# Spatial weights loaded from POOL's own queue, cast and subtraction in one step, and stacks held back around the change from z2 to z1

## The chip, the cores and the metric

The kernel runs on 1 core of a Trainium2 chip. The metric is device time in microseconds of one execution: before the change 1884.51 us, the median of 3 runs (1882.85 to 1885.61). The profile is of one further execution.

## The reference

The block adds attention and a gated MLP, both on the same layer norm, to its input. All data is fp32; S = 2048, D = 512, 32 heads of 16, F = 1792, Fh = 896.

```python
def _A_ref(x, wqkv, wo):                      # H = 32, Dh = 16
    q, k, v = split_heads(x @ wqkv)
    p = _softmax(jnp.einsum("bhqd,bhkd->bhqk", q, k) * (Dh ** -0.5))
    return merge_heads(jnp.einsum("bhqk,bhkd->bhqd", p, v)) @ wo

def _B_ref(x, w_in, w_sp, b_sp, w_out):
    z = _gelu(jnp.einsum("bsd,df->bsf", x, w_in))
    z1 = z[..., :Fh]
    z2 = _layernorm(z[..., Fh:], axis=-1)
    g = jnp.einsum("ts,bsf->btf", w_sp, z2) + b_sp[None, :, None]
    return jnp.einsum("bsf,fd->bsd", z1 * g, w_out)

xn = _layernorm(x)
return x + _A_ref(xn, A_wqkv, A_wo) + _B_ref(xn, B_w_in, B_w_sp, B_b_sp, B_w_out)
```

(`split_heads` and `merge_heads` stand for its reshapes.)

## The kernel before

Every fp32 operand is kept as a rounded part and a rest (`[128, 2, 512]`, fp32r), and a product is three matmuls. A raw weight of 128x512 is loaded, POOL casts it into the first part (L282) and subtracts that from the raw one into the second (L284).

After a start of some 125 us PE's work is written in 128 **rounds** by a `while` loop at the end of the kernel. Each round has 8 score slots (S, L1095; ACT takes their exponential, L71), 7 or 9 slots of maxima for a later head pair (M, L1109; DVE reduces each, L811), up to 27 **dense** slots (D, L1154), and one block of 32 values matmuls (V, L1192). A slot is a pair of matmuls on two halves of the array. The dense slots come from a queue in this order: v, q and k of the remaining heads, z2 (16 tiles of the second half of the MLP), z1 (its first half, 14 pairs), spatial (4 groups of 512 rows, each with 7 units over 16 weights wsp), mlp_out (with the 7 weights wout), attn_out (8 blocks of 24 slots with the weights wo). Where the loop's planner thinks that no dense slot is ready it writes a **filler** (F, L1168, products with zeros), or nothing.

The planner has a clock for PE and one each for ACT, DVE and POOL (`T["P"]`, `"A"`, `"D"`, `"G"`). A task is a generator: `yield "G", 0.61` books 0.61 us of POOL, and the instructions behind it are written when the planner's clock gets there; `"T"` is a delay (a load is taken to last LOAD = 5.0), `"C"` waits for a condition. So these numbers set the order of the instructions on every engine; how long things take on the chip does not enter. On the chip each engine takes its own instructions in order.

Buffers: a ring `big` of 19, for which the planner keeps leases; 3 of `hilo`; two accumulators in `dps` for the dense products, which the drain of a unit (L901 for attn_out) must read before the next may begin. At most DEEP = 4 raw weights are on their way at once. All transfers go out from SP (`move`, L125) in one order, but for the stores of xscr (L155), hscr (L722) and oscr (L870), which go out from POOL. `z2scr` holds z2 in DRAM; `zs` are its pieces, loaded again by SP for the spatial products. z1 is drained by ACT or DVE into `z`, to which POOL and ACT apply the gelu (L581 to L591, the tanh at L71). The outputs of the four groups of heads are normalized by `norm_out`: sums `os` (L851), their reciprocals stored to rscr and read back over all partitions (`ob`), POOL's products (L854, L858), the split (L864, L866) and the store to oscr. The last two head pairs' path ends in L934 to L956. `load_stacks` loads q and k of the next head pair.

Weights of one kind are asked for by `prepare`, which spawns a `weight` task for each.

Of the kernel before, what the change touches and what calls it, by code (L numbers as in the profile page):

```python
# [16 lines left out]
P = 128  # L17
# [5 lines left out]
NT = S // P  # L23
# [30 lines left out]
def fused_block(ctx, tc, x, wqkv, wo, w_in, w_spT, b_sp, w_out, out):  # L54
# [185 lines left out]
    def begin(nm, src, n, blocks=1, early=None):  # L240


        rw = piece(nm + "r").bitcast(F32)[:, 0, :n]
        dst, hi = rw, early
        if blocks > 1:
            src = src.rearrange("(c p) f -> p c f", p=P)
            dst = dst.rearrange("p (c f) -> p c f", c=blocks)
            hi = early and early[:, 0, :n].rearrange("p (c f) -> p c f", c=blocks)
        elif early:
            hi = early[:, 0, :n]  # L250
        move(dst, src)
        if early:
            nc.gpsimd.dma_start(hi, src)
        return rw
# [10 lines left out]
    def prepare(out, loads, spare=(0,)):  # L265
        for k, *a in loads:
            owed[0] += 1
            spawn(weight(out, k, a, spare), 1)
# [4 lines left out]
    def weight(out, k, a, spare):  # L273
        yield "C", lambda: raws[0] < DEEP and room["big"] > 1 + spare[0]
        raws[0] += 1
        rw = begin(*a)
# [4 lines left out]
        yield "G", 0.61  # L281
        nc.gpsimd.tensor_copy(t[:, 0, :n], rw)  # L282
        yield "G", 0.0026 * n
# [256 lines left out]
    def z2_all():  # L540
        yield from need(lambda: len(w2) == 2 * ND)
        for t in range(NT):
# [4 lines left out]
            if t == NT - 3:  # L547
                prepare(w1, [(f, f"w1_{f}", w_in[:, f * P:(f + 1) * P], D, ND) for f in range(NF)], spare=late1)
# [50 lines left out]
    def z1_all():  # L599
        for g in range(NG):  # L600
# [55 lines left out]
    def spatial():  # L656
        for n, (g, (x, y)) in enumerate(units):
# [7 lines left out]
            if lone:  # L665
                if g + 1 < NG:
                    prepare(wsp, [((g + 1, s), *sp_weights(g + 1, s)) for s in range(NT)])
                else:
                    prepare(wout, [(f, f"wout{f}", w_out[f * P:(f + 1) * P, :], 512) for f in range(NF)], spare=(2,))
# [118 lines left out]
    stacks = [0]  # L788

# [45 lines left out]
    def norm_out(g4, c):  # L835
# [16 lines left out]
        after(0.3, move, rscr[g4][c][:nh].rearrange("h (b x) -> h b x", x=32), sums[rows, 1, :])  # L852
# [124 lines left out]
    with tc.manual_schedule(engines=engines):  # L977
# [104 lines left out]
        def scores():  # L1082
# [5 lines left out]
            if p + 1 < NP and stacks[0] <= p and i >= (3 if p else 20) and (not owed[0] or i >= LATE):  # L1088
# [214 lines left out]
```

## Time and profile before

| | before |
|---|---|
| median of 3 runs | 1884.51 us (1882.85 to 1885.61) |
| the profiled execution | 1888.93 us, its span 1887.1 (1.8 lie around it) |
| mean granted clock of PE | 0.989 |
| PE busy | 1825.1 us (97%) |
| DVE, ACT, POOL busy | 1444.7, 1225.3, 690.7 us |
| DMAs issued by SP's and POOL's queues, share of the 16 engines | 50.6% and 4.8% |

A line of a group reads: line, engine, operation, out<-in with shapes and count, then busy us and mean ns of one, then the engine's idle time before it with what ended it. A row of a timeline reads: start, busy us, engine, line, operation, and in brackets the idle time just before. A row of a table by stretch reads: the stretch, its length, then busy us (and instructions) of the engines, the clock, the DMA share and GB/s. DMA lines end with the median us from issue to landing where the queue shows it. Buffer numbers are left out of names, so `wsp` is any spatial weight and `z` any of the MLP's first products.

### The profile page before, as it was taken

Reading aid. Unit: us, or ns where it says so; the run is one execution under the profiler, and the core shown is the slowest. Engines: PE = TensorE matmul, PEld = TensorE weight load, DVE = VectorE, ACT = ScalarE, POOL = GpSimd, SP = SyncE. Lnnn points to the kernel's source line nnn. Section 1 sums busy time; section 2 is a strip of 40 time slices with the busy share of each in tenths; the row PEclk is TensorE's granted clock in tenths of the full one; section 3 lists DMA queues with packets and bytes.
Section 4 is the critical chain, followed back from the end, with each engine's and each line's share of the span. In section 5 each row is a group of like instructions: output and inputs, shape, how many; then the busy total and the mean of one; then the engine's idle time right before and its main releaser. Section 6 shows DMA issues by size and latency. Waiting matters only on the chain.

```text
span 1887.1 us, 38105 instructions
## 1 busy us (share of the span) xinstructions
PE 1825.1 (97%) x14812; PEld 1109.3 (59%) x14812; DVE 1444.7 (77%) x1677; ACT 1225.3 (65%) x1338; POOL 690.7 (37%) x797
## 2 busy tenths in 40 slices
PE   6899999999998999999999999999999999999998
PEld 5665656566554656566655656565656565556554
DVE  5577878888876878778777877787778777878873
ACT  4247777888775777666656666666666665656555
POOL 2202142687886878800171217000722140002110
PEclk9899999999998999999999999999999999999999
DMA  9505573444455353474677657463787576456342
GB/s 329 208 3 170 203 225 111 98 137 118 133 160 160 129 130 110 141 167 119 158 201 194 165 142 227 133 148 103 219 194 160 161 201 145 124 140 174 116 129 92
DMA packets 208109, 291.47 MB, mean 154 GB/s; under 512 B 36008, under 2 KB 107368, under 8 KB 205048
## 3 DMA queue, kind: packets, MB, share of 16 engines
q1 hardware_dynamic: 197944, 258.03, 50.6%
q0 software_dynamic: 9984, 31.01, 4.8%
q8 instruction: 116, 1.90, 0.4%
q14 instruction: 65, 0.53, 0.1%
HBM read 186.98 MB, written 101.98 MB: 153 GB/s over the span
## 4 chain that ended last, share of the span: by engine, by line
PE 84%; DMA 4%; DVE 4%; POOL 4%; issue 2%; ACT 2%; SPq 0%; DVEq 0%; POOLq 0%; ACTq 0%
PE dps L1154 33%; PE sl L1192 22%; PE sl L1095 13%; PE sl L1109 12%; DVE mm L811 3%; DMA mscr<-ms 1%; PE dps L1168 1%; POOL wsp L284 1%; ACT pf L71 1%; DMA wqk<-in_wqkv 1%; PE sl L236 0%; PE sl L237 0%; DMA qst<-mscr 0%; PE sl L238 0%; ACT x L327 0%
## 5 line engine op out<-in xcount | busy, mean ns | idle before, releaser
L811 DVE TENSOR_REDUCE mm<-sl 128x2 f32<-128x1024 f32 x1024 | 1226.2, 1223 | 184.0 <-PE sl L1109 178.3
L71 ACT ACTIVATE pf<-sl 128x1024 f32<-128x1024 f32 x1024 | 1042.9, 1027 | 356.6 <-PE sl L1095 315.4
L1192 PE MATMUL sl<-pf,vall 128*32 128x512 f32 x4096 | 467.3, 597 | 0.0
L1095 PE MATMUL sl<-qst,kst 50*128 50x512 f32 x2048 | 441.4, 421 | 13.0 <-DVE mm L811 2.9
L1154 PE MATMUL dps<-wsp,zs 64*128 64x512 f32 x2688 | 441.4, 393 | 3.1 <-DMA zs<-z2scr 3.1
L1109 PE MATMUL sl<-kst,qst 48*128 48x512 f32 x2048 | 428.1, 408 | 7.2 <-DVE mm L811 3.5
L1095 PEld LDWEIGHTS sl<-qst,kst 50*128 50x128 f32 x2048 | 197.6, 185 | 223.8 <-issue 85.7
L1154 PEld LDWEIGHTS dps<-wsp,zs 64*128 64x128 f32 x2688 | 266.8, 187 | 41.5 <-DMA zs<-z2scr 3.7
L1192 PEld LDWEIGHTS sl<-pf,vall 128*32 128x32 f32 x4096 | 120.3, 110 | 270.6 <-issue 241.1
L1109 PEld LDWEIGHTS sl<-kst,qst 48*128 48x128 f32 x2048 | 197.6, 186 | 113.5 <-ACT pf L71 54.6
L1212 DVE TENSOR_TENSOR e<-sl,e 128x512 f32<-128x512 f32 x64 | 44.3, 692 | 174.3 <-PE sl L1192 133.8
L720 POOL TENSOR_TENSOR hhl<-z1i,hhl 128x512 fp32r<-128x512 f32 x28 | 35.8, 1290 | 332.3 <-ACT hhl L71 332.3
L71 ACT ACTIVATE e<-sl 128x512 f32<-128x512 f32 x64 | 38.3, 599 | 176.5 <-PE sl L1192 159.9
L1154 PE MATMUL dps<-w,xt 64*128 64x448 f32 x768 | 110.9, 369 | 2.3 <-ACT z L71 0.4
L1154 PE MATMUL dps<-wout,hp 64*128 64x512 f32 x672 | 111.5, 393 | 0.0
L858 POOL TENSOR_TENSOR ob<-ob 128x512 f32<-128x512 f32 (+1 forms) x16 | 20.6, 1288 | 181.9 <-DMA ob<-rscr 181.9
L1154 PEld LDWEIGHTS dps<-w,xt 64*128 64x128 f32 x768 | 73.9, 186 | 17.1 <-issue 8.0
L420 POOL TENSOR_TENSOR qkhl<-qr,qkhl 128x512 fp32r<-128x512 f32 x24 | 30.4, 1285 | 115.2 <-ACT qkhl L71 93.7
L1154 PEld LDWEIGHTS dps<-wout,hp 64*128 64x128 f32 x672 | 65.5, 187 | 9.1
L854 POOL TENSOR_TENSOR ob<-ob 128x512 f32<-128x512 f32 (+1 forms) x16 | 21.0, 1312 | 96.8 <-DMA ob<-escr 96.8
L1154 PE MATMUL dps<-xnT,wqk 64*128 64x512 f32 x288 | 47.4, 396 | 1.1 <-ACT vall L71 0.4
L1154 PE MATMUL dps<-wo,op 64*128 64x512 f32 x288 | 47.5, 407 | 0.6
(279 smaller groups left out, 1629.0 us busy)
## 6 DMA issues: line engine op xcount, KB each, us to landing
zs<-z2scr SPq DMA_DIRECT2D x192, 256.0 KB
escr<-e SPq DMA_DIRECT2D x60, 256.0 KB
hscr<-hhl POOLq DMA_DIRECT2D x28, 512.0 KB, 5.6
qst<-qscr SPq DMA_DIRECT2D x30, 384.0 KB
kst<-kscr SPq DMA_DIRECT2D x30, 384.0 KB
qscr<-qkhl SPq DMA_DIRECT2D x16, 512.0 KB
xscr<-xnT POOLq DMA_DIRECT2D x16, 512.0 KB, 4.5
kscr<-qkhl SPq DMA_DIRECT2D x16, 512.0 KB
```

What stands on the lines that cost most here:

```text
L71: return nc.scalar.activation(out, in_, func, **kw)
L284: nc.gpsimd.tensor_sub(t[:, 1, :n], rw, t[:, 0, :n].bitcast(F32))
L420: nc.gpsimd.tensor_sub(hl[:, 1, :], raw_, hl[:, 0, :].bitcast(F32))
L720: nc.gpsimd.tensor_sub(hl[:, 1, :], z1, hl[:, 0, :].bitcast(F32))
L811: nc.vector.tensor_reduce(mmax[g][:, :, t, kc], sl[k], AX.X, ALU.max)
L854: nc.gpsimd.tensor_add(both_[rows, 0, :], both_[rows, 0, :], both_[rows, 1, :])
L858: nc.gpsimd.tensor_mul(both_[rows, 0, :], both_[rows, 0, :], both_[rows, 1, :])
L1095: nc.tensor.matmul(sl[k][:, j, :], kst[p % 2][rows, kt * P:(kt + 1) * P], qst[p % 2][rows, c * 512:(c + 1) * 512], start=True, stop=True)
L1109: nc.tensor.matmul(sl[k][:, j, :], qst[p % 2][rows, tt * P:(tt + 1) * P], kst[p % 2][rows, kc * 512:(kc + 1) * 512], start=True, stop=True)
L1154: nc.tensor.matmul(dps[:, bank, :w], lhs, rhs, start=go, stop=stop)
L1192: nc.tensor.matmul(sl[k][cols:cols + VW, 0, :], vpack(kt + r, 2 * p + j), pf[:, j * 512:(j + 1) * 512], start=n == n_pv, stop=n == n_pv + ...
L1212: nc.vector.tensor_add(e, sl[k][:, 0, :], e)
```

## The change

Four edits. `weight` books the cast and the subtraction as one POOL step, so nothing comes between them; this holds for all prepared weights, w_in's too. Spatial weights of groups 1 to 3 and wout (55 loads) are loaded by `nc.gpsimd.dma_start`, with 0.7 us of POOL's clock for each, in place of SP's `move`. `calm` is off from z2's tile 13 to the second pair of z1, in which time stacks are loaded only from score step LATE = 24 on. The store of rscr in `norm_out` is due 1.5 us after its reciprocal in place of 0.3. The lines behind the edits move down by 3 to 7 (L282 is L286 after, L1095 L1102, L1109 L1116, L1154 L1161, L1168 L1175, L1192 L1199, L901 L908).

```diff
-    def begin(nm, src, n, blocks=1, early=None):
+    def begin(nm, src, n, blocks=1, early=None, put=None):
...
-        move(dst, src)
+        (put or move)(dst, src)
...
-    def weight(out, k, a, spare):
+    def weight(out, k, a, spare, own=False):
         yield "C", lambda: raws[0] < DEEP and room["big"] > 1 + spare[0]
         raws[0] += 1
-        rw = begin(*a)
+        if own:
+            lease("big", -1)
+            yield "G", 0.7
+            lease("big", 1)
+        rw = begin(*a, put=nc.gpsimd.dma_start if own else None)
         n = rw.shape[1]
         yield "T", LOAD
         yield open_("big")
         t = piece(a[0])
-        yield "G", 0.61
+        yield "G", 0.61 + 0.0026 * n
         nc.gpsimd.tensor_copy(t[:, 0, :n], rw)
-        yield "G", 0.0026 * n
         nc.gpsimd.tensor_sub(t[:, 1, :n], rw, t[:, 0, :n].bitcast(F32))
...
             if t == NT - 3:
+                calm[0] = False
                 prepare(w1, ...)
...
+                if n == 1:
+                    calm[0] = True
...
-                    prepare(wsp, [((g + 1, s), *sp_weights(g + 1, s)) for s in range(NT)])
+                    prepare(wsp, [((g + 1, s), *sp_weights(g + 1, s)) for s in range(NT)], own=True)
                 else:
-                    prepare(wout, ..., spare=(2,))
+                    prepare(wout, ..., spare=(2,), own=True)
...
+    calm = [True]
...
-        after(0.3, move, rscr[g4][c]..., sums[rows, 1, :])
+        after(1.5, move, rscr[g4][c]..., sums[rows, 1, :])
...
-            if p + 1 < NP and stacks[0] <= p and i >= (3 if p else 20) and (not owed[0] or i >= LATE):
+            if p + 1 < NP and stacks[0] <= p and i >= (3 if p else 20) and (i >= LATE or calm[0] and not owed[0]):
```

How the order moves, at three places. POOL, in the preparation of group 1's spatial weights, before; `wsp_3r` is the raw weight, `ob` and `z1i` belong to the norm and to a spatial result:

```order
L282 CAST wsp_3_10240<-wsp_3r 128x512
L284 TENSOR_TENSOR wsp_3_10240<-wsp_3r,wsp_3_10240 128x512
L282 CAST wsp_4_10314<-wsp_4r 128x512
L284 TENSOR_TENSOR wsp_4_10314<-wsp_4r,wsp_4_10314 128x512
L282 CAST wsp_5_10327<-wsp_5r 128x512
L282 CAST wsp_6_10346<-wsp_6r 128x512
L284 TENSOR_TENSOR wsp_5_10327<-wsp_5r,wsp_5_10327 128x512
L284 TENSOR_TENSOR wsp_6_10346<-wsp_6r,wsp_6_10346 128x512
L282 CAST wsp_7_10378<-wsp_7r 128x512
L858 TENSOR_TENSOR ob_0_9942<-ob_0_9942 128x512
L710 TENSOR_TENSOR z1i_6_10091<-z1i_6_10091,z1b_10374 128x512
L284 TENSOR_TENSOR wsp_7_10378<-wsp_7r,wsp_7_10378 128x512
```

And now (`hhl` is the split of a spatial result, hscr its store):

```order
L287 TENSOR_TENSOR wsp_3_10358<-wsp_3r,wsp_3_10358 128x512
L251 DMA wsp_4r<-in_w_spT 128x512
L251 DMA wsp_5r<-in_w_spT 128x512
L251 DMA wsp_6r<-in_w_spT 128x512
L251 DMA wsp_7r<-in_w_spT 128x512
L873 TENSOR_TENSOR ohl_0_10316<-ob_0_9913,ohl_0_10316 128x512
L877 DMA oscr<-ohl_0_10316 256x1x512
L716 TENSOR_TENSOR z1i_6_10193<-z1i_6_10193,z1b_10478 128x512
L286 CAST wsp_4_10504<-wsp_4r 128x512
L287 TENSOR_TENSOR wsp_4_10504<-wsp_4r,wsp_4_10504 128x512
L726 TENSOR_TENSOR hhl_6_10506<-z1i_6_10193,hhl_6_10506 128x512
L286 CAST wsp_5_10511<-wsp_5r 128x512
```

POOL now issues the loads in fours, between the subtraction of the last of one four and the cast of the first of the next.

ACT, where z1 begins, before: `z_0_0<-dps` drains z1's first product, `z2hl_0` rounds a piece of z2 into a `hilo` buffer, `pf` are exponentials:

```order
L71 ACTIVATE z2u_5768<-z2u_5768 128x896
L71 ACTIVATE pf_6112<-sl_188 128x1024
L71 ACTIVATE pf_6119<-sl_186 128x1024
L71 ACTIVATE pf_6129<-sl_187 128x1024
L71 ACTIVATE pf_6142<-sl_188 128x1024
L71 ACTIVATE pf_6154<-sl_186 128x1024
L71 ACTIVATE z2hl_0_6106<-z_14_5347,zrs_5757 128x512
L71 ACTIVATE pf_6163<-sl_187 128x1024
L71 ACTIVATE z_0_0_6165<-dps 128x512
```

And now:

```order
L71 ACTIVATE z2u_5768<-z2u_5768 128x896
L71 ACTIVATE z_0_0_6102<-dps 128x512
L71 ACTIVATE pf_6110<-sl_187 128x1024
L71 ACTIVATE pf_6122<-sl_188 128x1024
L71 ACTIVATE pf_6132<-sl_186 128x1024
L71 ACTIVATE pf_6150<-sl_187 128x1024
L71 ACTIVATE pf_6165<-sl_188 128x1024
L71 ACTIVATE pf_6182<-sl_186 128x1024
L71 ACTIVATE pf_6197<-sl_187 128x1024
L71 ACTIVATE pf_6214<-sl_188 128x1024
L71 ACTIVATE z_0_0_6102<-z_0_0_6102 128x512
L71 ACTIVATE z2hl_0_6181<-z_14_5347,zrs_5757 128x512
```

The drain stands seven rows earlier, ahead of the z2 piece and of the exponentials.

PE, the beginning of round 63, in the change from group 0 to 1, before:

```order
L1095 MATMUL sl_188<-qst_91,kst_93 128x512 x2
L1109 MATMUL sl_187<-kst_92,qst_90 128x512 x2
L1154 MATMUL dps<-wsp_0_10219,zs_10676 128x512 x6
L1154 MATMUL dps<-wsp_1_10225,zs_10676 128x512 x2
L1095 MATMUL sl_186<-qst_91,kst_93 128x512 x2
```

And now, where wsp_8 of the same group is the first that this round uses:

```order
L1102 MATMUL sl_187<-qst_91,kst_93 128x512 x2
L1116 MATMUL sl_188<-kst_92,qst_90 128x512 x2
L1175 MATMUL dps<-brow,zeror 128x512 x2
L1102 MATMUL sl_186<-qst_91,kst_93 128x512 x2
L1175 MATMUL dps<-brow,zeror 128x512 x4
L1116 MATMUL sl_187<-kst_92,qst_90 128x512 x2
L1102 MATMUL sl_188<-qst_91,kst_93 128x512 x2
```

Fillers stand where dense slots stood. In all, dense slots and fillers by round (other rounds up to 102 have at most 3 slots of difference, the same work overall):

| rounds | before: D (F) | after: D (F) |
|---|---|---|
| 30–34 | 2, 22, 8, 16, 24 (14, 0, 0, 0, 0) | 6, 18, 13, 15, 20 (12, 0, 7, 0, 1) |
| 46–52 | 25, 9, 10, 27, 26, 25, 24 (1, 7, 7, 1, 0, 0, 1) | 25, 9, 3, 12, 24, 24, 25 (2, 5, 10, 6, 1, 0, 0) |
| 62–69 | 24, 24, 24, 25, 24, 24, 24, 25 (1, 0, 0, 0, 1, 0, 0, 0) | 25, 9, 11, 17, 27, 27, 27, 27 (2, 7, 6, 3, 0, 0, 0, 0) |
| 77–81 | 24, 24, 25, 24, 24 (0, 0, 0, 1, 0) | 22, 12, 12, 27, 24 (2, 6, 6, 0, 0) |
| 92–99 | 24, 25, 24, 24, 24, 25, 24, 24 (2 in all) | 25, 9, 12, 16, 27, 27, 27, 27 (3, 8, 5, 4, 0, 0, 0, 0) |
| 123–127 | 17, 27, 4, 19, 18 (4, 0, 8, 3, 0) | 24, 24, 24, 24, 24 (none) |
| behind the last V | 11 (7) | 72 (7) |

mlp_out (21 slots a round) begins in round 103 before and 107 after, attn_out in 119 and 123. SP's rows go from 914 to 859, POOL's from 794 to 849; the stores of rscr and the loads of the stacks stand among the other rows of SP around z2's end as before.

More of the change, by code (lines that the diff above doesn't have):

```diff
@@ L851, in norm_out @@
         nc.vector.reciprocal(sums[rows, 1, :], sums[rows, 0, :])
-        after(0.3, move, rscr[g4][c][:nh].rearrange("h (b x) -> h b x", x=32), sums[rows, 1, :])
+        after(1.5, move, rscr[g4][c][:nh].rearrange("h (b x) -> h b x", x=32), sums[rows, 1, :])
         yield "G", 1.3
```

6 lines of the change are left out of this document (3 added, 3 removed).

## The prediction

> **What bounds the kernel now.** First the page: engine shares, the chain that ended last, and the costliest groups.
>
> ```profile
> PE 1825.1 (97%) x14812; PEld 1109.3 (59%) x14812; DVE 1444.7 (77%) x1677; ACT 1225.3 (65%) x1338; POOL 690.7 (37%) x797
> PE 84%; DMA 4%; DVE 4%; POOL 4%; issue 2%; ACT 2%; SPq 0%; DVEq 0%; POOLq 0%; ACTq 0%
> L811 DVE TENSOR_REDUCE mm<-sl 128x2 f32<-128x1024 f32 x1024 | 1226.2, 1223 | 184.0 <-PE sl L1109 178.3
> L1154 PE MATMUL dps<-wsp,zs 64*128 64x512 f32 x2688 | 441.4, 393 | 3.1 <-DMA zs<-z2scr 3.1
> ```
>
> PE holds 84% of the chain, and POOL is busy 37% of the span. So the edits on POOL pay only where PE waits for POOL's product, or where they change PE's own order. They do change it: the planner of the kernel reckons its order from costs of POOL steps. I therefore cut the trace at the ends of the 128 rounds and compare stretches. First, what a round costs when its dense slots are few (view: busy time by stretch, PE alone):
>
> ```profile
> 776.49:789.15 12.66, 12.32 (x98) 1.00 0.30 96
> 789.15:803.01 13.86, 13.65 (x104) 1.00 0.49 144
> 803.01:817.51 14.50, 14.38 (x122) 1.00 1.01 176
> 817.51:831.40 13.89, 13.89 (x122) 1.00 0.58 155
> 998.40:1011.38 12.98, 12.98 (x110) 1.00 0.34 93
> 1011.38:1025.04 13.66, 13.66 (x120) 1.00 1.02 210
> ```
>
> The first round has 7 maxima, 9 dense slots and 7 fillers, the second 9, 10 and 7; the third 7 maxima, 27 slots and a filler, the fourth 9 and 26. The last two are full rounds of 24 slots with 7 and 9 maxima. A round with 9 slots is only 0.3 us shorter than one with 24: the eight maxima on DVE (1223 ns each by L811's row) set a floor. **Dense slots that the planner leaves out of a round are thus not saved, they are postponed.** Prices from here: 12.7 to 13.0 (7 maxima) and 13.7 to 13.9 (9) for up to 25 slots; 13.6 and 14.1, my choice beside the 14.50 and 13.89 above, for 27.
>
> **Where PE now waits.** The worst stretch, rounds 30 to 34, and the change from spatial group 0 to 1, rounds 62 to 69 (columns: length, then busy us of PE, PEld, DVE, ACT, POOL, clock, DMA share):
>
> ```profile
> 533.76:613.09 79.33, 70.92 (x499) 36.17 (x496) 56.24 (x68) 49.98 (x57) 61.93 (x82) 0.89 0.54 152
> 762.07:858.50 96.43, 95.63 (x781) 55.91 (x778) 74.11 (x83) 61.36 (x65) 37.48 (x40) 1.00 0.56 142
> 978.89:1091.85 112.96, 109.56 (x908) 67.02 (x905) 85.52 (x98) 70.10 (x72) 29.62 (x30) 0.98 0.66 175
> 1186.31:1252.91 66.60, 66.46 (x563) 41.00 (x563) 50.55 (x53) 43.82 (x45) 4.19 (x4) 1.00 0.58 138
> 1387.99:1495.67 107.68, 107.41 (x904) 65.79 (x904) 85.53 (x98) 70.22 (x72) 24.01 (x23) 1.00 0.70 174
> 1806.42:1874.66 68.24, 64.27 (x534) 35.42 (x527) 29.87 (x36) 40.64 (x43) 6.24 (x6) 0.97 0.31 98
> 1874.66:1887.10 12.44, 7.46 (x72) 4.22 (x68) 7.77 (x8) 0.00 (x0) 0.00 (x0) 0.97 0.45 169
> ```
>
> What stands behind the first (timelines of SP, POOL, ACT, PE):
>
> ```profile
> 522.68 0.51 SPq L125 DMA_DIRECT2D w_0r<-in_w_in  x1
> 532.05 0.32 SPq L125 DMA_DIRECT2D rscr<-os  x1
> 532.47 1.06 SPq L125 DMA_DIRECT2D w_1r<-in_w_in  x1
> 568.62 0.68 POOL L870 DMA_DIRECT2D oscr<-ohl  x1
> 574.93 0.60 ACT L71 ACTIVATE z<-dps 128x512 f32<-128x512 f32 x1 [5.21 <-issue]
> 575.58 1.65 PE L1154 MATMUL dps<-xnT__5663,w 64*128 64x512 f32 x6 [4.44 <-ACT z L71]
> ```
>
> SP stands still between w_0r and w_1r, behind the rscr store; the weights reach POOL late, POOL's oscr store goes out at 568.62, and z_0_0 on ACT, whose buffer that store must free, starts at 574.93. PE waits 4.44 us. At 984 it is the z2 pieces and SP's queue:
>
> ```profile
> 986.76 0.50 PE L1154 MATMUL dps<-wsp,zs 64*128 64x512 f32 x1 [2.66 <-DMA zs<-z2scr]
> 988.07 1.49 PE L1154 MATMUL dps<-wsp,zs 64*128 64x512 f32 x6
> SPq L125 <- POOL wsp L284: 17.2, 7, 3.8
> ```
>
> The last row is SP's waits from 940 to 1000: in seven of them, 17.2 us, a raw load waited for a buffer that POOL's subtraction frees, and the zs loads queued behind it. This is what the loads on POOL's queue take away.
>
> **The change part by part, in time.** All differences are against the profiled execution (1888.93 us, 4.4 over the median of 1884.51); I carry the difference over to the median.
>
> *Rounds 30 to 34.* SP's order there is the same in both, rscr between w_0r and w_1r included, so that 9.4 us gap (522.68 to 532.05) stays, and with it the late POOL; the store moved by 1.2 us on the planner's clock changes nothing here. What goes is z_0_0's wait: ACT now has it seven rows earlier, on a buffer that is free; the z2 piece behind it takes the wait over, and late next are the exponentials behind that piece. By shape the five rounds now cost 13.9+12.9+13.9+12.7+13.7 = 67.1. Of the PE idle time in round 32 (6.57 us, 22.52 less the 15.95 in the row below) I leave half, 3.3: 70.4, that is **−8.9** (bounds −12.2 with no wait left, 0 if all stays).
>
> ```profile
> 560.68:583.20 22.52, 15.95 (x86) 0.70 0.90 224
> 565.12 0.66 PE L1095 MATMUL sl<-qst,kst 50*128 50x512 f32 x2 [0.48 <-DVE mm L811]
> 566.25 0.80 PE L1095 MATMUL sl<-qst,kst 50*128 50x512 f32 x2
> ```
>
> A part of that stretch is a slow clock, 0.70. The Trainium skill ("TensorE: Matmul & The Clock Gate", section "Why this matters for your kernels") says that TensorE drops to half rate after idle gaps of about 3 us, and advises to keep gaps shorter; by this the clock comes back with the gap of 4.44 us removed. The rows say something else: pairs take 0.66 and 0.80 us at 565 and 566, before that gap, and at 988 three slots take 1.49 after a gap of only 2.66. If the slowness stays, 30% of 15.95, 4.8 us, must be taken off the gain, which lies within the bound of 0 above: 1889.8 in place of 1885.
>
> *Rounds 46 to 52* lose 24 slots to later (D 9, 3, 12 in rounds 47 to 49): 14.4+12.7+13.9+12.8+13.7+13.0+13.9 = 94.4 for 96.43, **−2.0**. *Rounds 62 to 69* (25, 9, 11, 17, then four of 27): 13.9+12.7+13.9+12.9+14.1+13.6+14.1+13.6 = 108.8 for 112.96, **−4.2**: the wait at 984 goes, PE does fillers instead. *Rounds 77 to 81*: 66.7 for 66.60, **+0.1**. *Rounds 92 to 99*: as 62 to 69 but 14.1 for the first, 109.0 for 107.68, **+1.3**; nothing was waiting there. *Rounds 103 to 122*: the wout rounds stand four later, **−0.9** from the shorter attn_out rounds that leave.
>
> *The end.* Rounds 123 to 127 have 24 slots each and no late ob any more: 13.3+13.4+3×12.6 = 64.5 for 68.24, **−3.7**. But behind the last values block stand 72 dense slots, not 11:
>
> ```profile
> 1798.51 4.26 DMA ob<-rscr
> 1855.61 0.70 PE dps L1154 x6
> 1874.73 1.14 PE sl L949 x8
> 1879.44 1.23 DVE fin L901
> ```
>
> Three slots take 0.70, so 61 more take 14.2. The two accumulators of dps are read by L901 (1.23 us) between the blocks of 24, and there is nothing left to hide that: L949 (1.14) covers the first change, the second costs some 2 with its latencies. **+16.2**, bounds +14.2 and +19.
>
> *POOL's steps and loads.* Prices:
>
> ```profile
> 947.38 0.61 POOL L282 CAST wsp<-wsp_0r 128x512 fp32r<-128x512 f32 x1 [4.94 <-DMA wsp_0r<-in_w_spT]
> 948.08 1.29 POOL L284 TENSOR_TENSOR wsp<-wsp_0r,wsp 128x512 fp32r<-128x512 f32 x1
> 942.42 0.37 SPq L125 DMA_DIRECT2D wsp_0r<-in_w_spT  x1
> L722 POOL DMA_DIRECT2D hscr<-hhl x28 | 24.5, 890 | 0.7 <-POOL hhl L720 0.6
> hscr<-hhl POOLq DMA_DIRECT2D x28, 512.0 KB, 5.6
> oscr<-ohl POOLq DMA_DIRECT2D x12, 512.0 KB, 4.4
> wqk<-in_wqkv POOLq DMA_DIRECT2D x2, 256.0 KB, 9.9
> ```
>
> Cast and subtraction back to back take 2.0 us (947.38 to the end of the second at 949.37). 55 issues at 0.89 add some 49 us to POOL's 690.7, in idle time. But POOL works in order: four loads, four pairs, four loads. No load of the next four can go out until the pairs are done, and hhl's subtraction, the hscr store and ob stand behind a pair that waits for its load; spatial results wait for a hilo buffer there. One batch takes one issue, one landing and four pairs: 0.89+5.6+8.0 = 14.5 us with hscr's landing. The planner allots 0.7+5.0+4×1.94 = 13.5, so POOL falls 1 us behind its order in each batch, 4 us in a group of four batches. A landing like oscr's 4.4 or SP's own (942.42 to 947.38, 5.0) costs 0 to 1.6; one like wqk's 9.9, the only row with loads of this size on this queue, but from the kernel's start, would cost over 20 us a group. I take hscr's, the nearest in load, and a quarter of its 4 us, since fillers stand ahead of most batches' first use: **+3** in three groups; wout, two batches behind a long spatial unit, at 0.
>
> The Trainium skill ("DMA: Bandwidth & Descriptors", section "Latency and other measured facts") gives a first byte after some 1 us on GpSimd's software path against 0.6 on SP's; its section "Issuing engines are not separate DMA queues" says that all share the same 16 engines, so that another issuer saves only issue time. Added to SP's 5.0 that estimate is a landing of 5.4, and the term falls to about +2, 1884. The medians 4.4 and 5.6 lie on both sides of it.
>
> *Calm* moves no row: the stacks stand at the same place in SP's order, 0.
>
> Sum: −8.9−2.0−4.2+0.1+1.3−0.9−3.7+16.2+3 = +0.9, so 1889.8 for the profiled run and **1885** for the median. Put shortly: PE's order has 168 filler slots for 120, and 48 of them (11.2 us at 0.233) cost about what the waits that go were worth.
>
> **Rivals.** (1) *Faster.* The z_0_0 wait goes whole (−3.3) and weights are never late (−3): **1879**. For it speaks that the wait has one cause and that ACT's order removes it; against it the SP gap that stays. (2) *Slower: POOL's own loads are late.* With a DMA share of 0.66 to 0.70 in the changes of group, landings of 6.5 us give 1.9 a batch, 7.6 a group; half reaches PE, 11.4 for 3: **1893**. It decides from a landing of about 6 us on. For it speaks the wqk row, against it the two stores' medians. (3) *The stall of rounds 30 to 34 stays*, because POOL is as late as before and the next ACT row blocks as long: the −8.9 falls away, **1894**. (4) *The change doesn't do what it says*: SP's zs loads are late for other reasons, and PE waits at the same places as well as filling: the −4.2 and half of the −2.0 fall away, **1890**.
>
> **Chances.** Within 0.2% (3.8 us, about what a measurement of this kernel can tell from no change) is the forecast's own case, 1881 to 1888: 0.37. Rival 1: 0.28, all of it faster. Rival 2: 0.20, rival 3: 0.09, rival 4: 0.06, all slower: 0.35. The range takes rival 1 with the bound of no wait at all, 1876, and rivals 2 and 3 with the tail's upper bound, 1896.
>
> **What would show it.** Right: no gap above 3.3 us before L1154's successor (L1161) around 575; fillers (L1175) in rounds 63 to 65 and no wait for zs; last values block about 15 us earlier against the end than now, 28 to 29 us before it rather than 12.4; POOL's load issues of 0.7 to 0.9 us and landings near 5.6. Wrong: PE waits for wsp with POOL's cast as releaser above 1 us a group (rival 2), z_0_0's wait merely renamed (rival 3), or short rounds that really are shorter than 12.7, since then the postponed slots cost less than I charge.

## The result, and the profile after

| | before | after |
|---|---|---|
| median | 1885.06 us (1882.85 to 1887.52, 4 runs) | 1905.73 us (1903.06 to 1907.86, 4 runs) |
| ratio to before | | 1.0103 [1.0091, 1.0116] |
| profiled execution, its span | 1888.93, 1887.1 us | 1907.86, 1906.1 us |

The changed kernel is slower by 1.03%, about 20 us, where the prediction said no change (1885) with a range up to 1896. From the page of after, the engines, the chain, and two groups (the spatial products and the fillers):

```profile
PE 1843.6 (97%) x14908; PEld 1109.5 (58%) x14908; DVE 1440.9 (76%) x1677; ACT 1221.5 (64%) x1338; POOL 721.9 (38%) x852
PE 84%; DMA 5%; DVE 4%; POOL 2%; issue 2%; ACT 2%; SPq 0%; DVEq 0%; POOLq 0%; ACTq 0%
...
L1161 PE MATMUL dps<-wsp,zs 64*128 64x512 f32 x2688 | 437.4, 394 | 5.2 <-POOL wsp L286 3.9
...
L1175 PE MATMUL dps<-brow,zeror 64*128 64x512 f32 x336 | 62.4, 398 | 1.3 <-ACT z L71 0.7
```

The shares say almost nothing: PE is still 84% of the chain, POOL still under 40% busy. Two details speak. The spatial products, which before waited 3.1 us for z2's pieces, now wait for POOL's cast (`wsp L286`). And 336 filler matmuls, 168 slots, are in PE's order, as the forecast counted; the dense slots that they displaced were not saved but postponed.

Cut at the ends of the rounds, as in the prediction (before its numbers stand there; lengths in us, all from the profiled executions):

| rounds | before | after | difference | forecast |
|---|---|---|---|---|
| 30–34 | 79.33 | 78.72 | −0.6 | −8.9 |
| 46–52 | 96.42 | 93.73 | −2.7 | −2.0 |
| 62–69 | 112.96 | 119.34 | +6.4 | −4.2, and a share of +3 |
| 92–99 | 107.68 | 113.22 | +5.5 | +1.3, and a share of +3 |
| 103–122 | 269.88 | 269.66 | −0.2 | −0.9 |
| 123–127 | 68.24 | 66.68 | −1.6 | −3.7 |
| behind round 127 | 12.44 | 29.40 | +17.0 | +16.2 |

The rows by stretch of after: rounds 30 to 34, 62 to 69, and what lies behind round 127 (columns as before: length, PE, PEld, DVE, ACT, POOL, clock, DMA share):

```profile
531.29:610.00 78.71, 71.92 (x510) 37.04 (x506) 56.04 (x68) 48.87 (x55) 63.87 (x85) 0.93 0.55 151
972.96:1092.30 119.34, 113.18 (x893) 65.25 (x890) 83.74 (x96) 68.54 (x71) 49.94 (x55) 0.97 0.66 177
...
1876.70:1906.10 29.40, 22.98 (x194) 15.37 (x190) 10.14 (x10) 0.00 (x0) 0.00 (x0) 0.97 0.36 121
```

**Rounds 30 to 34.** ACT, then PE, in after:

```profile
577.14 0.81 ACT L71 ACTIVATE z2hl<-z,zrs 128x512 fp32r<-128x512 f32 x1 [3.81 <-DMA oscr<-ohl]
...
578.38 0.57 ACT L71 ACTIVATE e<-sl 128x512 f32<-128x512 f32 x1
```

```profile
575.56 0.63 PE L1161 MATMUL dps<-xnT__5665,w 64*128 64x512 f32 x4
579.00 0.50 PE L1102 MATMUL sl<-qst,kst 50*128 50x512 f32 x2 [2.81 <-ACT e L71]
```

z_0_0 no longer waits. The row behind it, `z2hl`, waits for the same oscr store (3.81 us), the exponential `e` stands behind it on ACT, and PE waits for that. The wait was renamed and moved one round on. How far one profiled execution can be trusted here: the kernel before and the two kernels with memsets below have the same order of instructions on every engine up to the end of round 34, and the five rounds took 79.33, 78.44 and 80.68 us.

**Round 63.** POOL in after, at the change from group 0 to 1:

```profile
958.47 1.27 POOL L865 TENSOR_TENSOR ob<-ob 128x512 f32<-128x512 f32 x1 [5.82 <-DMA ob<-rscr]
...
983.32 1.28 POOL L287 TENSOR_TENSOR wsp<-wsp_7r,wsp 128x512 fp32r<-128x512 f32 x1
984.55 0.58 POOL L251 DMA_DIRECT2D wsp_8r<-in_w_spT  x1
...
995.20 1.26 POOL L861 TENSOR_TENSOR ob<-ob 128x512 f32<-128x512 f32 x1 [8.46 <-DMA ob<-escr]
996.41 0.61 POOL L286 CAST wsp<-wsp_8r 128x512 fp32r<-128x512 f32 x1
...
1019.60 1.28 POOL L287 TENSOR_TENSOR wsp<-wsp_15r,wsp 128x512 fp32r<-128x512 f32 x1
```

and PE:

```profile
997.07 2.15 PE L1161 MATMUL dps<-wsp,zs 64*128 64x512 f32 x6 [3.91 <-POOL wsp L286]
```

In fours, as the order showed: wsp_8 is asked for at 984.55, when before POOL was about to finish the last one:

```profile
986.67 1.27 POOL L284 TENSOR_TENSOR wsp<-wsp_15r,wsp 128x512 fp32r<-128x512 f32 x1
```

In after, wsp_15 is done at 1020.88 (1019.60 and 1.28), 33 us later than the 987.94 of before. Between load and cast of wsp_8 stands an `ob` product, which holds POOL for 8.46 us until its read has landed; the weight lies ready behind it and PE stands. The first four of the group stood behind such a row too (958.47, 5.82 us). POOL is not busy in these two waits, it is held by its order.

**The end.** PE behind the last values block, in after:

```profile
1888.08 2.34 PE L1161 MATMUL dps<-wo,op 64*128 64x512 f32 x18
1890.26 0.85 PE L1161 MATMUL dps<-wo,ohl 64*128 64x512 f32 x6
1892.43 2.35 PE L1161 MATMUL dps<-wo,op 64*128 64x512 f32 x18 [1.33 <-DVE fin L908]
```

72 dense slots stand here instead of 11. Nine slots take 2.34, 0.26 each, so 61 more take 15.9, and the change of accumulator costs 1.33 at L908: 17.2 for a measured 17.0.

### The profile page after: what moved, and what is told of

Its sections match the earlier page's. It is cut to its first block, busy times and chain, and to the rows that moved or that the text cites. A ratio compares the mean times of both kernels' runs of the same rounds, so it can differ in the third digit from the quotient of the medians.

```text
span 1906.1 us, 38247 instructions
## 1 busy us (share of the span) xinstructions
PE 1843.6 (97%) x14908; PEld 1109.5 (58%) x14908; DVE 1440.9 (76%) x1677; ACT 1221.5 (64%) x1338; POOL 721.9 (38%) x852
## 4 chain that ended last, share of the span: by engine, by line
PE 84%; DMA 5%; DVE 4%; POOL 2%; issue 2%; ACT 2%; SPq 0%; DVEq 0%; POOLq 0%; ACTq 0%
PE dps L1161 34%; PE sl L1199 22%; PE sl L1102 13%; PE sl L1116 12%; DVE mm L818 3%; DMA zs<-z2scr 1%; PE dps L1175 1%; DMA kst<-in_wqkv 1%; DMA ob<-escr 1%; DMA oscr<-ohl 1%; DMA qst<-qscr 1%; ACT pf L71 1%; ACT x L330 0%; DMA rscr<-os 0%; POOL w L287 0%
## 5 line engine op out<-in xcount | busy, mean ns | idle before, releaser
L1199 PE MATMUL sl<-pf,vall 128*32 128x512 f32 x4096 | 467.7, 597 | 0.1
L1102 PE MATMUL sl<-qst,kst 50*128 50x512 f32 x2048 | 440.9, 423 | 13.1 <-DVE mm L818 3.6
L1161 PE MATMUL dps<-wsp,zs 64*128 64x512 f32 x2688 | 437.4, 394 | 5.2 <-POOL wsp L286 3.9
L1116 PE MATMUL sl<-kst,qst 48*128 48x512 f32 x2048 | 426.3, 409 | 7.9 <-ACT pf L71 3.7
L1102 PEld LDWEIGHTS sl<-qst,kst 50*128 50x128 f32 x2048 | 195.6, 184 | 229.3 <-issue 87.5
L1161 PEld LDWEIGHTS dps<-wsp,zs 64*128 64x128 f32 x2688 | 261.4, 187 | 48.9 <-POOL wsp L286 4.3
L1199 PEld LDWEIGHTS sl<-pf,vall 128*32 128x32 f32 x4096 | 120.4, 110 | 271.6 <-issue 243.8
L1116 PEld LDWEIGHTS sl<-kst,qst 48*128 48x128 f32 x2048 | 196.0, 185 | 117.4 <-ACT pf L71 63.5
L1161 PE MATMUL dps<-w,xt 64*128 64x448 f32 x768 | 110.7, 369 | 2.3 <-ACT z L71 0.4
L1161 PE MATMUL dps<-wout,hp 64*128 64x512 f32 x672 | 111.4, 392 | 0.0
L1161 PEld LDWEIGHTS dps<-w,xt 64*128 64x128 f32 x768 | 73.5, 186 | 17.5 <-issue 8.0
L1161 PEld LDWEIGHTS dps<-wout,hp 64*128 64x128 f32 x672 | 65.5, 187 | 8.9
L1175 PE MATMUL dps<-brow,zeror 64*128 64x512 f32 x336 | 62.4, 398 | 1.3 <-ACT z L71 0.7
L1161 PE MATMUL dps<-xnT,wqk 64*128 64x512 f32 x288 | 47.3, 396 | 1.1 <-ACT vall L71 0.4
```

The source lines that it names most:

```text
L1102: nc.tensor.matmul(sl[k][:, j, :], kst[p % 2][rows, kt * P:(kt + 1) * P], qst[p % 2][rows, c * 512:(c + 1) * 512], start=True, stop=True)
L1116: nc.tensor.matmul(sl[k][:, j, :], qst[p % 2][rows, tt * P:(tt + 1) * P], kst[p % 2][rows, kc * 512:(kc + 1) * 512], start=True, stop=True)
L1161: nc.tensor.matmul(dps[:, bank, :w], lhs, rhs, start=go, stop=stop)
L1175: nc.tensor.matmul(dps[:, bank, :], zeror[r:r + 64], brow[r:r + 64], start=not begun, stop=not begun)
L1199: nc.tensor.matmul(sl[k][cols:cols + VW, 0, :], vpack(kt + r, 2 * p + j), pf[:, j * 512:(j + 1) * 512], start=n == n_pv, stop=n == n_pv + ...
```

## The experiments

POOL is the engine that the theories differ on. One says that in the changes of group POOL's time sets when PE gets its weights, so that each load issued on POOL costs PE time; the others put the loss on late landings, on the order in which POOL is written, or on the stall of rounds 30 to 34. Below, "merge" is the cast and the subtraction booked as one step, and a "late slot" is a dense slot behind the last values block. All ratios are to the kernel before on the same chip, whose medians were 1885.2 to 1886.3 us.

### Without the loads on POOL's queue

```diff
-    prepare(wsp, [...], own=True)
+    prepare(wsp, [...])
-    prepare(wout, [...], spare=(2,), own=True)
+    prepare(wout, [...], spare=(2,))
```

> All of the change but the loads on POOL's own queue: SP issues every raw load again. PE's order has 134 filler slots (120 before, 168 with the whole change) and no dense slot behind the last values block (11, 72). Theory 1, the time goes into postponed dense slots, since the booked POOL step in front of each load lets the loads go out only in fours behind the casts: the tail's 17 us and the waits of rounds 63, 67 and 97 go, 1877 to 1886. Theory 2, it goes into the single step of cast and subtraction, which holds up the rest of POOL's queue: still above 1895.

1885.6 us, 0.9996 [0.9983, 1.0009]. As the first theory had it. Merge, calm and the later rscr together make no difference that can be measured; the 20 us belong to the loads on POOL and the step booked for them. The end is short again: there are 134 fillers, and no late slot; behind round 127 lie 12.88 us. Rounds 62 to 69 take 110.03 us (119.34 with the loads) and rounds 92 to 99 106.50 (113.22). But the stall of round 32 is in round 33 here too, so it does not come from the loads:

```profile
575.70:598.34 22.64, 17.89 (x97) 9.23 (x94) 9.50 (x11) 12.09 (x15) 15.09 (x22) 0.70 0.57 154
```

The merge itself gives and takes: rounds 62 to 74 are 3.0 us shorter than before, 75 to 102 are 7.6 longer, since SP's loads now wait for whole pairs on POOL (10.6 us for `wsp L287` from 1340 to 1391) and zs behind them.

### Loads on POOL, with no booked step ahead of them

```diff
-        if own:
-            lease("big", -1)
-            yield "G", 0.7
-            lease("big", 1)
```

> The whole change, but a load on POOL's queue is written at once when the planner asks for it, without the booked step of 0.7 and without waiting for POOL's clock. POOL's order then has a load behind each pair of cast and subtraction, not four behind four; PE's order is that of the kernel without own loads (134 fillers, none of the dense slots in the tail). Theory 1 (order): 1873 to 1884, since SP's waits for POOL at the change of groups go as well. Theory 2 (landings on POOL's own queue are late, 6 us and more): PE waits for wsp at each change of groups, 1890 to 1900.

1910.66 us, 1.0133 [1.0118, 1.0148]. The planner no longer knows of POOL's issue time, there are no fours, 134 fillers and no late slots, and it is worse than the change and above both expectations. The loss now lies in the waits of the three changes of group (rounds 62 to 74, 75 to 88, 89 to 102):

```profile
974.42:1164.24 189.82, 180.47 (x1479) 110.23 (x1475) 139.22 (x159) 112.63 (x117) 64.24 (x71) 0.97 0.70 176
1164.24:1362.82 198.58, 192.05 (x1589) 117.08 (x1585) 147.73 (x162) 121.19 (x126) 54.72 (x64) 0.97 0.53 142
1362.82:1562.78 199.96, 192.54 (x1589) 117.60 (x1585) 150.29 (x170) 121.24 (x126) 74.18 (x84) 0.97 0.69 175
```

Together they take 588.36 us, against 562.25 in the first experiment with the same order of PE. So the loss does not need the fours and the late slots: without them it appears as waiting.

### The same, with cast and subtraction apart

```diff
-        yield "G", 0.61 + 0.0026 * n
+        yield "G", 0.61
         nc.gpsimd.tensor_copy(t[:, 0, :n], rw)
+        yield "G", 0.0026 * n
```

> As the kernel before, with PE's order the same slot for slot (120 fillers, 11 dense slots in the tail), but the spatial and wout loads go out from POOL's queue at the same place of the planner's clock; cast and subtraction are two steps as before, calm and the later rscr store stay in. It shows what the queue itself does. Theory 1: only the wait at 984 us in round 62 goes, 1878 to 1883. Theory 2 (late landings, POOL's time for issues): slower than before, 1890 or more.

1900.56 us, 1.0078 [1.0061, 1.0095]. PE's order is now that of before, slot for slot, and so is that of ACT, of DVE and of POOL but for the loads; what differs is where 55 loads are issued, and on SP the places of rscr and of some loads of stacks (the section on the rscr store comes back to these). POOL in the preparation of group 2:

```profile
1145.39 0.56 POOL L251 DMA_DIRECT2D wsp_5r<-in_w_spT  x1 [0.30 <-POOL wsp L284]
1145.98 1.30 POOL L284 TENSOR_TENSOR wsp<-wsp_2r,wsp 128x512 fp32r<-128x512 f32 x1
```

An issue is 0.56 us of POOL, and 0.30 more where it waits for the subtraction right ahead to finish. The rest of POOL's rows stand back to back: there is no idle time for the issues to lie in.

### The loads alone, with the booked step

The change without the merge, calm and rscr edits:

```diff
-        yield "G", 0.61 + 0.0026 * n
+        yield "G", 0.61
         nc.gpsimd.tensor_copy(t[:, 0, :n], rw)
+        yield "G", 0.0026 * n
...
-        after(1.5, move, rscr[g4][c]..., sums[rows, 1, :])
+        after(0.3, move, rscr[g4][c]..., sums[rows, 1, :])
...
-            if ... and (i >= LATE or calm[0] and not owed[0]):
+            if ... and (not owed[0] or i >= LATE):
```

> The own loads alone with their booked step of 0.7, cast and subtraction in two steps, no calm, rscr store as before. 144 filler slots, 48 dense slots behind the last values block. Theory 1: the price goes by the postponed slots, so about half of the way from before to after by fillers and two thirds by the tail: 1893 to 1901. Theory 2 (the single step costs): about as before, 1882 to 1889.

1894.9 us, 1.0056 [1.0041, 1.0071], within the first theory's range: 9 to 11 us, about half of the loss. 144 fillers, and 48 dense slots behind round 127, where 22.76 us now lie. The merge alone is neutral and the loads alone cost some 9 us; together they cost 20.

### POOL's time alone, and doubled

To the kernel before, two (then four) memsets of an otherwise unused 128x64 tile on POOL for each of the 55 weights, where SP's load is issued. The loads stay on SP, and PE's order is that of before.

```diff
+    idle = cp.tile([P, 64], F32, name="idle")
...
+        if a[0][:3] in ("wsp", "wou") and a[0][:4] != "wsp0":
+            for i in range(2):          # second kernel: range(4)
+                nc.gpsimd.memset(idle, 0.0)
         rw = begin(*a)
```

> The kernel before with its loads on SP, and only two small memsets of a scratch tile on POOL where each of the 55 loads of groups 1 to 3 and of wout is asked for (an estimate of 0.5 to 0.6 us together by the 0.19 us and 0.27 us spacing of the tiny zrs operations; the loads in the run with unqueued own loads and two steps took 0.56, some with 0.3 more). They compute nothing that is used; PE's order is that of before. Theory A, POOL's own time at the change of groups is the cost: as that run, 1894 to 1902, with PE's waits in rounds 62, 75, 76, 89 and 90. Theory B, the landing on POOL's queue or the transfers' order is the cost: 1884 to 1889.

> As the run with two memsets on POOL for each load, with four: about 0.62 us of POOL for each of the 55 weights (two took 0.31), which is what an own load took of POOL in the run with unqueued own loads and two steps (0.56, some 0.3 more). Loads stay on SP, PE's order is that of before. Theory A, POOL's time at the change of groups has a slack of some 5 us a group and costs its full length beyond: 3 x 5 more than the two memsets, 1898 to 1904. Theory B, POOL's time is not it but the wait of a load in POOL's queue and the later buffers: 1888 to 1893.

1888.87 us, 1.0015 [1.0004, 1.0025], and 1903.77 us, 1.0093 [1.0078, 1.0108]. By its total the first fell to theory B; but two memsets were also shorter than a load (by the sums below 9.6 us of POOL for 48 weights, 0.2 each, where the loads took 23.2). The second, which matches the loads in POOL's time, fell to theory A. Four memsets, from the first start to the last end:

```profile
1151.83 0.78 POOL L280 MEMSET idle<- 128x64 f32 x4
```

The three changes of group (rounds 62 to 74, 75 to 88, 89 to 102) together, as the sum of three rows by stretch; it gives the length, then the busy time of each engine. Before:

```profile
sum 557.65, PE 552.62 PEld 337.19 DVE 438.31 ACT 358.37 POOL 163.05; mean PE 184.21 PEld 112.40 DVE 146.10 ACT 119.46 POOL 54.35
```

With two memsets:

```profile
sum 562.92, PE 556.31 PEld 340.41 DVE 438.39 ACT 358.22 POOL 172.64; mean PE 185.44 PEld 113.47 DVE 146.13 ACT 119.41 POOL 57.55
```

With four:

```profile
sum 574.40, PE 558.23 PEld 340.74 DVE 438.51 ACT 358.17 POOL 187.04; mean PE 186.08 PEld 113.58 DVE 146.17 ACT 119.39 POOL 62.35
```

And with the loads on POOL, unqueued, cast and subtraction apart:

```profile
sum 574.12, PE 560.31 PEld 341.38 DVE 438.57 ACT 358.37 POOL 186.23; mean PE 186.77 PEld 113.79 DVE 146.19 ACT 119.46 POOL 62.08
```

POOL's busy time grows by 9.6, 24.0 and 23.2 us, the three stretches by 5.3, 16.8 and 16.5. Four memsets, with no load moved, give what the moved loads give: the single stretches grow by 3.4, 7.1 and 6.3 us with the one and by 3.3, 6.3 and 6.8 with the other. Two kernels below that keep PE's order of before (the later rscr store without the merge, with the shorter and the longer calm) differ from before by at most 2.3 us in a stretch. So landings, queues and PE's order are not needed to explain that loss; POOL's time suffices, at 0.55 to 0.7 us of the stretches for each us of POOL. POOL is busy 163 of 558 us here, 29%, and still the bound: the 16 weights of a group, 2 us each, stood in before between 947 and 988 with four waits, 4.1 us in all, between them.

### Booked ahead of the planner's clock

```diff
-            yield "G", 0.7
+            gps(0.7)
```

The 0.7 us are added to POOL's planned time, but the load is not queued behind other POOL steps.

> The whole change, but the load is written at once and 0.7 us is put on POOL's clock, without queueing behind POOL's other work: the planner knows of the time and loads do not go in fours. 141 filler slots, none of the dense slots in the tail. Theory A (POOL's time): PE still waits at each change of groups, since POOL's order is the same as without the booking, but part of it is filled with work: 1896 to 1908. Rival (what hurt was only that the planner did not know): 1880 to 1888.

1893.75 us, 1.0051 [1.0034, 1.0067], between the two expectations. 141 fillers, and nothing late at the end: of the change's 20 us, 10 to 13 come from the queued form of the step, which makes the fours and the late slots, and 7 to 10 remain with POOL's time booked (the smaller remainder by the medians, the larger by the ratio). That remainder needs no fours: rounds 62 to 69 take 119.30 us here too.

### Another buffer for the store in rounds 30 to 34

The first experiment, with the split of one norm piece in the ring instead of `hilo`, so that no `z2hl` can wait for its store:

```diff
-        if g4 < 3:
+        ring = g4 == 3 or (g4, c) == (0, 1)
+        if not ring:
...
-        hl = piece(...) if g4 == 3 else hilo(...)
+        elif g4 < 3:
+            yield open_("big")
+        hl = piece(...) if ring else hilo(...)
...
-            after(3.5, lease, "hilo", 1)
+            after(3.5, lease, "big" if ring else "hilo", 1)
```

> The change without own loads, and the one norm output (group 0, quarter 1) whose store held z2's piece up at 573 us is put into a buffer of the ring in place of one of the three hilo buffers. Theory: the wait of ACT for the oscr store was what moved from z_0_0 to z2hl; rounds 30 to 34 fall from 80.3 to 67 to 72 us and the time to 1872 to 1879, faster than both kernels. Rival: the transfers (stacks, z2, norm) saturate the queues there, another wait takes its place, rounds 30 to 34 stay at 78 to 80 and the time at 1883 to 1887.

1888.89 us, 1.0014 [1.0004, 1.0023], worse than both expectations. The five rounds take 82.33 us. Waits from 575 to 600:

```profile
PE dps L1164 <- DVE z L579: 5.9, 1, 5.9
ACT z L71 <- DMA z2scr<-z2hl: 5.6, 1, 5.6
```

The wait is renamed once more: with the oscr store out of the way, ACT waits as long for the store of z2's piece. One buffer is not the cause.

### The rscr store behind the weights

SP's gap between w_0r and w_1r comes from the rscr store that stands there. Due 4.0 us after its reciprocal, it moves behind the weights: to the kernel before (with calm as in the change), then with the merge as well, then with the merge for all weights but those of groups 1 to 3 and wout.

```diff
-        after(0.3, move, rscr[g4][c]..., sums[rows, 1, :])
+        after(4.0, move, rscr[g4][c]..., sums[rows, 1, :])
```

> The kernel before with the rscr store due 4.0 us after its reciprocal (0.3 before, 1.5 in the change), so that on SP it stands behind w_1r, w_2r and w_3r, not ahead of them; calm stays in, everything else as before and PE's order the same slot for slot. Theory: SP's 9.4 us wait there is the root of the stall of rounds 30 to 34, so POOL's casts and the oscr store come 6 to 9 us earlier: rounds 30 to 34 at 68 to 73 us for 79.3, total 1875 to 1881. Rival: the three hilo buffers and the transfers of 560 to 580 us set the stall: 76 to 80 us, total 1882 to 1888.

1882.12 us, 0.9982 [0.9972, 0.9991]: faster than both kernels, but within the rival's range. SP in this kernel:

```profile
519.82 0.44 SPq L125 DMA_DIRECT2D w_0r<-in_w_in  x1
525.29 0.38 SPq L125 DMA_DIRECT2D w_1r<-in_w_in  x1
```

From w_0r to w_1r it is now 5.5 us, where it was 9.8, and rounds 30 to 34 take 77.33 for 79.33. That is less than the cause should have given: the wait is in round 34 now, for a z2 store (waits from 588 to 608):

```profile
ACT z L71 <- DMA z2scr<-z2hl: 3.0, 1, 3.0
```

And the edit moves more than the text of the expectation says. With cast and subtraction apart, the calm of the change does move stacks on SP. The first load of the next head pair's q in this stretch, before, in the change, here, and in the kernel with unqueued loads and cast and subtraction apart:

```profile
562.51 0.49 SPq L125 DMA_DIRECT2D qst<-qscr  x1
561.08 0.48 SPq L125 DMA_DIRECT2D qst<-qscr  x1
573.35 0.39 SPq L125 DMA_DIRECT2D qst<-qscr  x1
575.16 0.40 SPq L125 DMA_DIRECT2D qst<-qscr  x1
```

The last of these still has rscr between w_0r (521.52) and w_1r (531.24), 9.7 us apart, and the same order on the other engines up to there. Its five rounds:

```profile
532.56:608.18 75.62, 71.49 (x498) 36.56 (x495) 56.29 (x68) 50.19 (x57) 61.80 (x82) 0.91 0.57 159
```

No row of PE waits longer than 1.1 us in them, and none for a store. So loading the stacks 13 us later, with rscr still ahead of w_1r, did what the rscr store was moved for; the 4 us of this experiment can't be put down to the rscr store alone.

> The change without own loads and with the rscr store due 4.0 us after its reciprocal, behind w_3r on SP. PE's order is that of the change without own loads. Theory as for the kernel before with that store: rounds 30 to 34 from 80.3 to 68 to 73, total 1873 to 1879. Rival: 1884 to 1888.

1884.47 us, 0.9990 [0.9981, 1.0000], five rounds 79.21: the rival. Here the stacks have not moved (562.50), and ACT still waits 4.5 us for the oscr store.

```diff
-        yield "G", 0.61 + 0.0026 * n
-        nc.gpsimd.tensor_copy(t[:, 0, :n], rw)
+        if own:
+            yield "G", 0.61
+            nc.gpsimd.tensor_copy(t[:, 0, :n], rw)
+            yield "G", 0.0026 * n
+        else:
+            yield "G", 0.61 + 0.0026 * n
+            nc.gpsimd.tensor_copy(t[:, 0, :n], rw)
```

> As the one before, but cast and subtraction are one step only for the weights of z1 and of spatial group 0; those of groups 1 to 3 and wout keep two steps and SP's queue. 133 filler slots, none of the dense slots in the tail. If the single step holds up hhl and z1i in the changes of groups 1 to 3 (rounds 75 to 102 took 384.9 with it, 377.3 before), this gives 3 to 7 us: 1868 to 1876. If that came from the places of the rounds and not from the step, as the one before, within 2 us.

1888.0 us, 1.0009 [0.9996, 1.0022]. A miss: the merge was kept where it had seemed to help and taken out of groups 1 to 3, yet rounds 62 to 74 take 184.2 us against 177.0 with the full merge. What the merge does in a stretch depends on the order as a whole; it can't be kept by pieces. The five rounds took 75.91 us, where the kernel just before, with the same order on all five engines up to there, took 79.21: 3.3 us between two executions of one order.

### A longer calm

Calm stays off until the first pair of group 1 of z1, so that the stacks that stood in rounds 32 to 34 load later (from 605.54, with the merge from 601.52); without and with the merge, rscr behind the weights in both.

```diff
-                if n == 1:
+                if g == 1 and n == 0:
                     calm[0] = True
```

> The kernel before with the rscr store behind w_3r, as in the earlier run of that kind, and calm kept off until z1's rows 512 to 1023 begin (in the change it is on again with the second pair of z1, which is before the step at which the next stacks may be loaded). On SP the stacks of the next head pair now stand some 12 rows later, behind the z2 stores of tile 14; PE's order is that of before. Theory, the stacks' loads make z2's stores late: rounds 30 to 34 from 77.3 to 68 to 72 us, total 1874 to 1879. Rival, three hilo buffers and POOL's in-order work set it whatever the transfers: 76 to 79, total 1881 to 1885; or the stacks then come late for the scores, which costs up to what is won.

1882.89 us, 0.9982 [0.9971, 0.9992]; five rounds:

```profile
533.71:608.89 75.18, 71.28 (x498) 36.62 (x494) 56.35 (x68) 50.06 (x57) 61.81 (x82) 0.91 0.45 136
560.67:578.93 18.26, 16.21 (x86) 7.37 (x82) 13.43 (x18) 10.49 (x12) 16.71 (x20) 0.72 0.47 147
```

> The change without own loads, rscr store behind w_3r, and the same longer calm. Theory: rounds 30 to 34 from 79.2 to 68 to 73, total 1874 to 1880. Rival: 78 to 80, 1883 to 1888.

1882.06 us, 0.9985 [0.9974, 0.9996]; five rounds:

```profile
530.17:604.41 74.24, 70.07 (x511) 35.95 (x508) 55.90 (x68) 49.22 (x55) 64.04 (x85) 0.95 0.44 136
```

By its total the first is the rival's case, the second lies between theory and rival. With a calm that covers the stacks, the DMA share of the stretch falls from 0.54 to 0.45 and five rounds cost 75.2, then 74.2. The waits for stores are gone (the longest wait of PE in round 32 is 1.0 us, for an exponential). The clock of round 32 is still 0.72. Without the merge this is hardly shorter than the 75.62 of the shorter calm, and the kernel as a whole gains nothing further by it: the intervals of the three fastest overlap.

## Why the prediction was wrong

**The steps that failed.** The forecast paid for the late slots (+16.2) with waits that were to go. The late slots came, the waits stayed. Three terms of the sum were wrong: −8.9 for rounds 30 to 34, −4.2 for rounds 62 to 69, and +3 for all that the loads would cost on POOL, which rests on "55 issues at 0.89 add some 49 us to POOL's 690.7, in idle time".

**POOL's time.** The added time was smaller than 49 us (POOL's busy time grew by 31.2 us; a load of 256 KB takes 0.54 to 0.69 us to issue, not the 0.89 of a 512 KB store), but in the order of before there is no idle time under it where it counts. POOL's 37% is a mean over the span; in the stretch before each spatial group its rows stand nearly back to back, and this was to be seen in the trace of before, from 947 to 988. Four memsets per weight reproduce the loss. I had priced only the exposed landing of a four, +3 in all. These experiments have the order of before. In the change, where the loads are booked, the same 55 loads cost late slots and the wait of round 63; how much of that is POOL's time and how much the order of its rows, no run separates.

The landings were mispriced too. I called wqk's 9.9 us the only row of loads of 256 KB on this queue; the same view has two more, 12.1 and 13.8, for q and k from the kernel's start. The medians of the 16 spatial weights are 3.5 to 9.0 us, seven of them above the 6 from which rival 2 counted.

The Trainium skill ("DMA: Bandwidth & Descriptors", section "Issuing engines are not separate DMA queues") says that another issuer saves only the sequencer's time for starting a transfer, and that this is usually small beside the transfer. The runs agree with both: with the loads off SP the three changes of group take as long as with memsets and the loads on SP (574.12 and 574.40), and an issue is 0.56 us beside landings of 3.5 to 9.0. But small is not free where the issuer is the bound: 0.56 us on POOL, 55 times, cost 14 us with PE's order unchanged (1900.56 against 1886.15).

**Rounds 62 to 69: −4.2 forecast, +6.4 measured.** I let the fillers replace the wait at 984. They did not: the order has the fillers, and the wait came back under another name, rival 2's, `wsp` by POOL's cast, 3.91 us. It came once, in group 1; in rounds 92 to 99 no row of PE waits longer than 0.4 us. Its cause was not rival 2's late landing. The cast of wsp_8 had no wait of its own; it stood behind an `ob` product that waited 8.46 us for its own read. The landing of wsp_8 took 8.3 us. So it was there at 992.9, later than the 5.6 that I took, but 3.5 us before the cast at 996.41; POOL's order decided, not the landing. Round 63 took 19.4 us where its shape was priced at 12.7: the wait, and half speed behind it (last section).

**Rounds 30 to 34: −8.9 forecast, −0.6 measured.** Rival 3, to which I gave 0.09. I had the SP gap and the late oscr store in hand, saw that both stay, and still took off half the idle time. Its mechanism was named in the rival: the next ACT row blocks as long. The change without its loads, the store from another buffer and the later rscr with the merge each move the wait by a round or a name and keep most of it. It is gone in the three kernels that load the stacks later and have no wait for a store above 0.4 us left (75.62, 75.18, 74.24 us), one of them with the SP gap as it was; so the gap that I took for its root is not needed for it. What this is worth is some 3 to 6 us of the five rounds by single executions, of which two with one order differed by 3.3, and not 8.9.

**Right:** the end (+16.2, measured +17.0; a slot there takes 0.26 and not 0.233, and the second change of accumulator 1.33 and not 2); that postponed slots are not saved; rounds 46 to 52; that the calm of the change moves no stacks in its own order (561.08 for 562.51), though it does where cast and subtraction are apart; that the rscr store at 1.5 us stays between w_0r and w_1r.

In sum +0.9 was forecast and +19.0 measured between the spans: of the 18.1 between them, 8.3 come from rounds 30 to 34, 9.6 from rounds 62 to 69 (with a third of the 3 for weights) and 3.2 from rounds 92 to 99 likewise; the other rounds take 3.0 back, 2.5 of it before round 30. What stays open is how the rest divides when loads and merge meet: alone they cost 9 and 0 us, together 20. The fillers and the late slots (48 against 72 behind the last round) show part of it; no experiment separates the remainder.

## What to carry to other kernels

An engine's share of the span says little on a stage: before putting work on an engine that is "37% busy", read its timeline just ahead of the consumer that waits for it, and if the rows stand back to back, price the added work in full. To test such a bound, add idle work of the same length to that engine and move nothing else. And before a wait is counted as gain, follow what made the producer late; a wait whose cause stays is only renamed.

## What the runs showed of the hardware

The granted clock of PE fell to half after gaps shorter than I had thought. Rows by stretch of after, behind the wait of 3.91 us in round 63, and behind the one of 2.81 us in round 33:

```profile
996.50:999.00 2.50, 1.81 (x6) 1.00 (x8) 0.00 (x0) 0.00 (x0) 2.34 (x4) 0.52 0.03 5
999.00:1003.30 4.30, 4.30 (x24) 3.35 (x22) 2.22 (x2) 2.05 (x2) 4.14 (x5) 0.50 0.18 61
1003.30:1008.18 4.88, 4.88 (x44) 1.74 (x40) 1.46 (x2) 2.03 (x2) 4.73 (x7) 0.99 0.50 156
580.30:583.40 3.10, 3.10 (x18) 2.33 (x14) 2.21 (x2) 1.51 (x2) 2.83 (x3) 0.50 0.72 241
```

From the end of the wait at 997.07 to 1003.4 PE works at half speed: an estimate from these rows is that the wait of 3.91 us costs another 3 behind it. No single long gap is needed. In the kernel before, the clock in round 32 fell behind waits of 0.22, 1.08, 0.17 and 0.48 us, one soon after the other, the last of them in the prediction's own row at 565.12; PE's rows fill half of the 3.41 us before the fall:

```profile
561.89:565.30 3.41, 1.67 (x10) 0.67 (x10) 2.29 (x3) 3.19 (x4) 3.41 (x5) 1.00 0.91 245
565.30:568.71 3.41, 3.36 (x12) 1.33 (x10) 3.04 (x3) 2.65 (x4) 3.41 (x4) 0.50 1.05 201
```

In all fifteen traces the clock changes only between full and half, and each stretch between two changes lasts a multiple of 3.41 us (13.65 here). Cut into such steps, from 100 us on, every step at full clock in which PE's rows fill less than half is followed by one at half, and none in which they fill more than three quarters; between these both occur. So the share of PE's time in such a step tells more than the length of one gap.

The Trainium skill ("TensorE: Matmul & The Clock Gate", section "HAM oscillation — how this bites in real kernels") gives the abstract rule as idle gaps over about 3.4 us; the half speed agrees, the length of a single gap does not, for here 2.81 us and a row of shorter ones sufficed.
